# Convolution and mixture of experts on one core: a pair's result goes from ScalarE to DRAM by an adding transfer, in a new order

## The chip, the cores and the metric

The program runs on one of the eight cores of a Trainium2 chip. The metric is device time in microseconds (us) of one execution. Engines are named as in the profile: PE (TensorE, matrix products), PEld (its weight loads), DVE (VectorE), ACT (ScalarE), POOL (GpSimd), SP (SyncE, which issues most DMA transfers).

## What is computed

A causal convolution with weights that differ from token to token, and a layer of eight experts behind it, over 8 x 3584 = 28672 tokens of 192 features:

```python
w = exp(weight_gen - max); w = w / (sum(w) + 1e-9)      # 8 heads, 7 taps per token
out = einsum('bshk,bskhg->bshg', w, x_unf)              # x_unf: the 7 last tokens, 24 features a head

skip_score = x @ w_skip                                 # x is the convolution's result
do_compute = skip_score > 0
logits = x[do_compute] @ w_gate                         # 8 experts
e_idx, gate_w = argmax(logits), softmax(logits)[e_idx]
out[do_compute] = x + gate_w * (relu(x @ w1[e]) @ w2[e])    # 192 -> 1024 -> 192
```

About half of the tokens go to an expert, the others keep the convolution's result.

## The kernel before

The tokens are cut into 16 chunks of 1792. In a chunk (`chunk`), the weights are loaded, normalised by a softmax (`soft`, units so, ss, sf, sm) and written to DRAM in a skewed image, from which they come back as rows (`rot`). `band` (unit bd, L437) multiplies them with a mask into band matrices, eight in a chunk; each may be made by VectorE or by GpSimd. `conv` (cv, L452) multiplies the bands with the inputs, `conv_out` (co, L459) copies the results out, `back` and `back_out` transpose them into a tile `acc`, which goes to the result tensor `out` in DRAM (`answer`). `logits`, `choose` (begins at L501), `rank` and `place` route the tokens: each active token's number is put into a list of its expert by `list_out` (L637, L638) and `send` (L647), an indirect transfer that adds 44 short rows to a table in DRAM.

A pair is two tiles of 128 tokens of one expert. For each of the 57 pairs (`pair`, class `Pair`) the steps are: `rows` (its 256 token numbers come from the table), `index` (L802, numbers to row indices; entries without a token get an index out of bounds and are skipped), `gather` (L809, two indirect transfers from `out` to a buffer `xg`, of which there are seven), `sums`, `scales`, `high`, `low` (L844), `cross` (L850), which split the rows into two float16 parts, a transposition (by TensorE for the first twelve pairs, by DMA from SP for the others), `up` (L880, four steps), `up_high` (hh, L885, ScalarE) and `up_low` (hl, L889, VectorE), `down` (L902, four steps), and then

```python
def finish(self):                       # L907, two instructions on VectorE
    nc.vector.scalar_tensor_tensor(xg, py, fc, xg, op0=mult, op1=add)
def scatter(self, t):                   # L911, two plain indirect transfers
    nc.gpsimd.indirect_dma_start(out=..., in_=xg, ...)
```

So a pair's rows are read, changed in `xg` and written back, and `xg` is taken again when that write has landed. Forty pairs are dealt out while chunks are still running, in batches (`BATCH`: after which chunk, for which experts), nine more by what is left of whole tiles, eight for the remainders. A loop at the end takes further tiles if there are any; in this run there are none. Each expert's weights are loaded and split into two float16 parts once (`expert`; split by L361 on ScalarE and L359 on VectorE).

No instruction finds its place at run time. A planner (`Planner`, `Paced`) runs when the kernel is built: each unit has an engine or a choice of engines, an estimated length, predecessors and buffers, and the unit with the smallest start plus a kind's bias from the table `LATER` is put next; each engine then works its list in order, and waits at its head for what it needs. `E_AT` says behind which input load an expert's weights are loaded, `AHEAD`, `LEAD` and `SWITCH` how far the convolution may run ahead of the pairs.

## Time and profile before

| | us |
|---|---|
| median of 3 runs | 921.68 (918.16 to 921.82) |
| profiled execution, its own time | 921.96 |
| its span, first to last instruction | 920.3 |
| TensorE busy | 778.9 (85%) |
| VectorE busy | 692.9 (75%) |
| ScalarE busy | 441.2 (48%) |
| GpSimd busy | 435.8 (47%) |
| mean granted TensorE clock, share of full speed | 0.925 |

The shares are means over a front in which convolution, routing and the first pairs run together and a last part of pairs alone. So the views that follow are cut by time. Matmuls are pipelined: a group's mean duration is longer than the step from one matmul to the next, and the step of a pair is read from time marks.

### The profile page before, as it was taken

How to read it: one execution, taken by the hardware profiler on the slowest of the kernel's cores; microseconds unless marked ns; L12 is line 12 of the kernel's file. 1: busy time of each engine (PE TensorE's matmuls, PEld its weight loads, DVE VectorE, ACT ScalarE, POOL GpSimd, SP SyncE). 2: the span in 40 equal slices, each digit the busy share in tenths (PEclk: the TensorE clock that was granted, in tenths of full speed). 3: DMA queues.
4: the chain of work that ended last, by engine and by line, in shares of the span. 5: the costliest groups of instructions: out<-in, count | busy, mean ns of one | idle time of the engine just before them, and what ended most of it. 6: DMA issues, size and time to landing. Idle time of an engine off the chain costs nothing. (4 is left out here: it accounts for less than half of the span.)

```text
span 920.3 us, 27436 instructions
## 1 busy us (share of the span) xinstructions
PE 778.9 (85%) x11064; PEld 682.7 (74%) x11064; DVE 692.9 (75%) x1822; ACT 441.2 (48%) x1028; POOL 435.8 (47%) x496
## 2 busy tenths in 40 slices
PE   2476767687597888979988899999999999999995
PEld 1365645466475767767867789999999999999995
DVE  6678988999998979988888686765656565656552
ACT  1345445555664566545644543444444444444441
POOL 2025336317544554964676426355545454446422
PEclk9677888689878879999999999999999999999998
DMA  4789688659663685566667544333334654995220
GB/s 135 202 243 318 214 301 279 200 159 381 176 192 116 209 300 167 168 224 201 220 211 208 174 112 94 70 88 88 74 81 82 152 147 121 250 273 142 65 46 21
DMA packets 107633, 158.80 MB, mean 173 GB/s; under 512 B 65734, under 2 KB 87190, under 8 KB 104560
## 3 DMA queue, kind: packets, MB, share of 16 engines
q1 hardware_dynamic: 95280, 135.28, 49.5%
q0 software_dynamic: 12224, 21.75, 8.4%
q8 instruction: 87, 1.43, 0.6%
q14 instruction: 42, 0.34, 0.1%
HBM read 88.07 MB, written 42.37 MB: 142 GB/s over the span
## 5 line engine op out<-in xcount | busy, mean ns | idle before, releaser
L889 DVE SCALAR_TENSOR_TENSOR hl<-h,hh 128x512 f16<-128x512 f32 x228 | 155.4, 686 | 136.8 <-ACT hh L885 136.6
L885 ACT ACTIVATE hh<-h 128x512 f16<-128x512 f32 x228 | 135.7, 597 | 227.4 <-PE h L880 221.7
L880 PE MATMUL h<-xT,held 128*128 128x256 f16 x1920 | 237.3, 276 | 0.0
L880 PEld LDWEIGHTS <-held 128*128 128x128 f16 x1920 | 187.0, 99 | 25.5 <-issue 3.9
L902 PE MATMUL py<-held,hh 128*128 128x192 f16 x1536 | 205.5, 248 | 0.0
L452 PE MATMUL h<-bd,xt 128*48 128x56 f32 x4096 | 145.1, 236 | 63.0 <-DVE bd L437 36.5
L911 POOL DMA_INDIRECT out_dram<-xg,idx x114 | 118.7, 1041 | 159.2 <-DVE xg L907 138.5
L452 PEld LDWEIGHTS h<-bd,xt 128*48 128x48 f32 x4096 | 130.8, 142 | 84.9 <-DVE bd L437 42.2
L902 PE MATMUL py<-held,hl 128*128 128x192 f16 x768 | 190.3, 248 | 2.3 <-DVE hl L889 2.3
L437 POOL TENSOR_TENSOR bd<-rot,mask 128x896 f32<-128x896 f32 x57 | 112.9, 1994 | 145.0 <-PE h L452 144.5
L902 PEld LDWEIGHTS <-hh 128*128 128x128 f16 x1824 | 166.1, 98 | 6.0 <-issue 1.8
L809 POOL DMA_INDIRECT xg<-out_dram,idx x114 | 122.9, 1078 | 90.5 <-issue 52.1
L459 ACT COPY xs<-h 112x448 f32<-112x448 f32 x123 | 65.2, 532 | 109.3 <-PE h L452 107.2
L902 PEld LDWEIGHTS <-hl 128*128 128x128 f16 x912 | 89.8, 98 | 3.8 <-DVE hl L889 3.6
L437 DVE TENSOR_TENSOR bd<-rot,mask 128x896 f32<-128x896 f32 x71 | 77.1, 1118 | 9.4 <-PE h L452 5.3
L468 PE MATMUL pa<-ident,xs 112*112 112x112 f32 x512 | 76.2, 286 | 9.4 <-ACT xs L459 7.6
L482 ACT COPY acc<-pa 112x384 f32<-112x384 f32 x128 | 57.3, 480 | 38.8 <-PE pa L468 35.9
L468 PEld LDWEIGHTS pa<-ident,xs 112*112 112x112 f32 x512 | 55.4, 145 | 20.0 <-ACT xs L459 13.2
L647 POOL DMA_INDIRECT table<-ly,lri x16 | 33.5, 2091 | 48.5 <-DVE ly L638 46.3
L907 DVE SCALAR_TENSOR_TENSOR xg<-py,fc,xg 128x192 f32<-128x192 f32 x114 | 41.9, 408 | 10.6 <-PE py L902 10.6
L839 ACT ACTIVATE xs<-xg,rs 128x192 f16<-128x192 f32 x114 | 44.9, 446 | 6.3 <-DVE rs L835 6.3
L470 PE MATMUL pa<-xs,gt 112*32 112x224 f32 x512 | 39.4, 381 | 9.3 <-ACT acc L482 8.3
(191 smaller groups left out, 956.0 us busy)
## 6 DMA issues: line engine op xcount, KB each, us to landing
xt<-in_x_dram SPq DMA_DIRECT2D x64, 768.0 KB
out_dram<-acc SPq DMA_DIRECT2D x16, 1351.0 KB
acc<-held SPq DMA_DIRECT2D x9, 1536.5 KB
held<-in_moe_w_dram SPq DMA_DIRECT2D x14, 768.0 KB
rot<-img SPq DMA_DIRECT2D x15, 448.0 KB
wt<-in_weight_gen_dram SPq DMA_DIRECT2D x15, 392.0 KB
img<-wt SPq DMA_DIRECT2D x30, 196.0 KB
xg<-out_dram,idx POOLq DMA_INDIRECT x114
```

The source lines that it names most:

```text
L437: (nc.gpsimd if on_pool else nc.vector).tensor_tensor(bd.rearrange("p h (m u) -> p h m u", m=K), rot_[c][:, :, i0 * H:(i0 + 2) * H].rearra ...
L452: nc.tensor.matmul(bt_[k][g][HR * j:HR * j + 2 * G, c0:c0 + QH], xt_[k][:, b0:b0 + 2 * G], bd_[k, i // 2][:, i % 2 * H + h, :], start=True ...
L459: (nc.scalar.copy if on_act else nc.vector.tensor_copy)(xs[:, 2 * g:2 * g + 2, :], bt_[k][g][0:Q, 0:2 * QB * QH].rearrange("p (x c) -> p x ...
L468: nc.tensor.transpose(t[0:Q, x * P:x * P + Q], xs[:, x, j * Q:(j + 1) * Q], ident[0:Q, 0:Q])
L482: nc.scalar.copy(acc_[c].rearrange("p (a b) d -> p a b d", a=2)[:, :, 2 * q + j, 0:D].rearrange("p a (x g) -> p a x g", g=G), t[0:Q, :].re ...
L809: i = nc.gpsimd.indirect_dma_start(out=self.xg[:, t, :], out_offset=None, in_=out[0:n, :], in_offset=bass.IndirectOffsetOnAxis(ap=self.idx ...
L839: nc.scalar.activation(self.xs[:, t, 0, 0:D], self.xg[:, t, 0:D], AF.Copy, scale=self.rs[:, t:t + 1])
L880: nc.tensor.matmul(ph[:, fi * 2 * P:(fi + 1) * 2 * P], self.fetched()[:, a * FF + f0:a * FF + f0 + P], self.xT[:, :, cc, :], start=j == 0, ...
L885: nc.scalar.activation(self.hh[f2], self.ph[f2], AF.Relu)
L889: nc.vector.scalar_tensor_tensor(self.hl[f2], self.ph[f2], 0.0, self.hh[f2], op0=ALU.max, op1=ALU.subtract)
L902: nc.tensor.matmul(self.py[:, t, 0:D], l[:, a], w2v[:, f, r, :], start=f == 0 and t == 0 and j == 0, stop=f == NFB - 1 and j == 2, skip_gr ...
L911: i = nc.gpsimd.indirect_dma_start(out=oviews[nsc[0] % 8], out_offset=bass.IndirectOffsetOnAxis(ap=self.idx[:, t:t + 1], axis=0), in_=self ...
```

## The change

`finish` becomes two ScalarE instructions that write the product of `py` and the factor `fc` alone to a buffer `y` (three of them, their 193rd column zero), and `scatter` adds `y` to the rows in DRAM: the transfers have compute_op=add. `xg` is only read, and is free after `low` and `factor`. Entries without a token no longer have an index out of bounds: `out` gets 1152 spare rows in front (`FIRST`), which are cleared once (`clear_rows`, 889 KB); a gather reads row p of them in partition p, and an addition goes to one of eight further blocks of 128. For this `index` makes two lists on VectorE, `idx` and `put`, and the small memset that GpSimd made in front of each pair's gathers goes. `BATCH`, `E_AT`, `LATER`, `AHEAD`, `LEAD`, `SWITCH` get other values and a list `PACE` ties late bands to early pairs, so all engines' lists are in a new order.

```diff
-BATCH = [(0, 0, 2), (0, 2, 4), (3, 4, 6), (5, 6, 8), (5, 0, 2), ...
+BATCH = [(4, 0, 2), (4, 2, 4), (4, 4, 6), (6, 6, 8), (6, 0, 2), ...
-E_AT = [8, 16, 18, 26, 5, 19, 38, 37]
+E_AT = [24, 0, 31, 20, 15, 35, 0, 10]
-LATER = ({"an": -0.77, "as": 1.7, "bd": 0.87, ...
+LATER = ({"an": 3.18, "as": 0.55, "bd": 1.91, ...
-AHEAD, LEAD, SWITCH, TURN = 3, 1, 14, 12
+AHEAD, LEAD, SWITCH, TURN = 6, 4, 25, 12
...
-    for t in xgs:
-        nc.gpsimd.memset(t, 0.0)
...
+    ys = [cst.tile([P, TT, RW], F32, name=f"y{i}") for i in range(NY)]
+    for y in ys:
+        nc.vector.memset(y[:, :, D:RW], 0.0)
...
         def index(self):
-            self.idx = sl.tile([P, TT], I32, tag="idx", name="idx", bufs=XG)
-            nc.vector.tensor_scalar(self.idx, self.ids, -1.0, BIG, op0=ALU.mult, op1=ALU.add)
+            self.idx = sl.tile([P, TT], I32, tag="idx", name="idx", bufs=16)
+            nc.vector.tensor_scalar(self.idx, self.ids, which, None, op0=ALU.max)
+            self.put = sl.tile([P, TT], I32, tag="put", name="put", bufs=16)
+            nc.vector.tensor_tensor(self.put, self.ids, spare_rows[:, self.view():self.view() + TT], op=ALU.max)
 
         def gather(self, t):
             self.xg = xgs[(self.p or 0) % XG]
-            if not t:
-                nc.gpsimd.memset(self.xg[:, :, D:RW], 0.0)
...
         def finish(self):
+            self.y = ys[(self.p or 0) % NY]
             for t in range(TT):
-                nc.vector.scalar_tensor_tensor(self.xg[:, t, 0:D], self.py[:, t, 0:D], self.fc[:, t:t + 1],
-                                               self.xg[:, t, 0:D], op0=ALU.mult, op1=ALU.add)
+                nc.scalar.activation(self.y[:, t, 0:D], self.py[:, t, 0:D], AF.Copy, scale=self.fc[:, t:t + 1])
 
         def scatter(self, t):
             i = nc.gpsimd.indirect_dma_start(
-                out=oviews[nsc[0] % 8],
-                out_offset=bass.IndirectOffsetOnAxis(ap=self.idx[:, t:t + 1], axis=0),
-                in_=self.xg[:, t, :], in_offset=None, bounds_check=N - 1, oob_is_err=False)
+                out=oviews[self.view() + t],
+                out_offset=bass.IndirectOffsetOnAxis(ap=self.put[:, t:t + 1], axis=0),
+                in_=self.y[:, t, :], in_offset=None, bounds_check=FIRST + N - 1, compute_op=ALU.add)
...
+    def clear_rows():
+        nc.sync.dma_start(out[0:FIRST, :].rearrange("(p r) c -> p r c", p=P), zeros[:, 0:RW].unsqueeze(1).to_broadcast([P, FIRST // P, RW]))
...
-        add(("fi", p), "DVE", .82, o.finish, [("dn", p, 3), ("fc", p)], gives=[("y", p, 1), ("fc", p, 1)])
+        add(("fi", p), "ACT", .85, o.finish, [("dn", p, 3), ("fc", p)], takes=["yy"], gives=[("y", p, 1), ("fc", p, 1)])
...
-                size=108, gives=[("xg", p, 2)])
+                size=108, gives=[("yy", p, 2)])
...
+        for h, n in enumerate(PACE):
+            if n:
+                behind(("bd", 2 * h, 0), ("up", n - 1, 0))
```

What the lists look like. Counted in TensorE's list, 1.75 pairs' up-products stand in front of the logits of the seventh chunk and 12 in front of those of the sixteenth before; now it is none and 20.5. Of the 128 bands VectorE makes 71 and GpSimd 57 before, now 33 and 95; up to the seventh routing VectorE makes 36 of them before and 27 now. Up to VectorE's seventh routing four experts' scales stand in its list before, two now. The numbers of lines differ between the two kernels: the finish is L907 and L919, the scatter L911 and L922, a band L437 and L445, the table L647 and L655, the gather L809 and L820.

GpSimd, in the chunks near the end of the convolution, before (bands, the table's transfer, the result's, the gathers):

```order
L437 TENSOR_TENSOR bd<-rot,mask 128x896 x2
L647 DMA table<-ly,lri 3870x64
L850 COPY xs<-xs 128x2x64 x2
L911 DMA out_dram<-xg_149,idx 28672x193 x2
L437 TENSOR_TENSOR bd<-rot,mask 128x896
L807 MEMSET xg_147 128x2
L809 DMA xg_147<-out_dram,idx 128x193 x2
```

and now, at the same place:

```order
L445 TENSOR_TENSOR bd<-rot,mask 128x896
L655 DMA table<-ly,lri 3870x64
L820 DMA xg_156<-out_dram,idx 128x193 x2
L922 DMA out_dram<-y_167,put 29824x193
L445 TENSOR_TENSOR bd<-rot,mask 128x896
L922 DMA out_dram<-y_167,put 29824x193
L445 TENSOR_TENSOR bd<-rot,mask 128x896 x3
```

A pair's two result transfers now read a `y` buffer and stand between bands, the memset is gone, and there are more bands on this engine.

ScalarE, up to the last chunk's exponential (L548) before; xs are the convolution's results, acc and ls their transposed copies, hh the first part of a pair's hidden values:

```order
L459 COPY xs_7913<-h_83 112x448
L850 COPY xs<-xs 128x2x64 x2
L482 COPY acc<-pa 112x2x192 x2
L478 COPY ls<-pa 128x224
L459 COPY xs_8010<-h_84 112x448
L459 COPY xs_8010<-h_85 112x448
L885 ACTIVATE hh<-h_83 128x512
L482 COPY acc<-pa 112x2x192 x2
L478 COPY ls<-pa 128x224
L885 ACTIVATE hh<-h_84 128x512
L885 ACTIVATE hh<-h_85 128x512
L548 ACTIVATE dls<-dls 112x16x8
```

and now, in the same chunk:

```order
L467 COPY xs_9003<-h_84 112x448
L919 ACTIVATE y_165<-py,fc 128x192 x2
L490 COPY acc<-pa 112x2x192 x2
L467 COPY xs_9100<-h_85 112x448
L467 COPY xs_9100<-h_83 112x448
L486 COPY ls<-pa 128x224
L896 ACTIVATE hh<-h_84 128x512
L490 COPY acc<-pa 112x2x192 x2
L896 ACTIVATE hh<-h_85 128x512
L486 COPY ls<-pa 128x224
L467 COPY xs_9250<-h_83 112x448
L467 COPY xs_9250<-h_84 112x448
```

The finish (L919) stands among the copies, in front of the next pair's hh.

VectorE, in a chunk of the second half before, with a pair's finish (L907) behind two bands:

```order
L844 SCALAR_TENSOR_TENSOR xs<-xg_147,rs,xs 128x192 x2
L939 SCALAR_TENSOR_TENSOR sent<-base,ecap 1x8
L437 TENSOR_TENSOR bd<-rot,mask 128x896 x2
L907 SCALAR_TENSOR_TENSOR xg_150<-py,fc,xg_150 128x192 x2
L832 TENSOR_SCALAR S_7643<-S_7643 128x2
L833 TENSOR_SCALAR S_7643<-S_7643 128x2
L835 RECIPROCAL rs<-S_7643 128x2
L870 SCALAR_TENSOR_TENSOR fc<-S_6667,held,xg_153 128x2
```

and now, just ahead of a routing, with no finish and with two index lists for a pair:

```order
L855 SCALAR_TENSOR_TENSOR xs<-xg_151,rs,xs 128x192 x2
L861 COPY xs<-xs 128x2x64 x2
L813 TENSOR_SCALAR idx<-ids,which 128x2
L815 TENSOR_TENSOR put<-ids,spare_rows 128x2
L509 TENSOR_SCALAR ina<-route,noob 112x16
```

The bands and the finish have left this part of the list.

## Rows read from the trace of the kernel before

**Rows 1.** Busy us per engine in three stretches, then granted clock, DMA share, GB/s.

```profile
55.26:233.26 178.00, 131.10 (x2390) 102.72 (x2387) 160.03 (x390) 94.51 (x192) 80.51 (x81) 0.84 0.78 261
233.26:532.43 299.17, 249.83 (x4330) 208.32 (x4329) 261.13 (x630) 167.84 (x384) 170.15 (x178) 0.91 0.61 196
532.43:900.00 367.57, 365.94 (x3868) 344.86 (x3867) 230.42 (x708) 162.80 (x425) 175.35 (x206) 1.00 0.49 117
```

**Rows 2.** The same view for one window of 46 us.

```profile
414.00:460.00 46.00, 42.37 (x762) 35.68 (x762) 40.80 (x105) 27.55 (x69) 24.64 (x30) 0.96 0.66 210
```

**Rows 3.** VectorE in order of time: start us, us, line; first, seventh, sixteenth routing.

```profile
55.26 0.23 DVE L501 TENSOR_SCALAR ina<-route,noob 112x16 f32<-112x16 f32 x1
...
233.26 0.23 DVE L501 TENSOR_SCALAR ina<-route,noob 112x16 f32<-112x16 f32 x1 [0.46 <-PE route L492]
...
532.43 0.23 DVE L501 TENSOR_SCALAR ina<-route,noob 112x16 f32<-112x16 f32 x1 [0.32 <-PE route L492]
```

**Rows 4.** The same view: the finish of the 15th and of the last pair.

```profile
560.47 0.74 DVE L907 SCALAR_TENSOR_TENSOR xg<-py,fc,xg 128x192 f32<-128x192 f32 x2
...
910.35 0.74 DVE L907 SCALAR_TENSOR_TENSOR xg<-py,fc,xg 128x192 f32<-128x192 f32 x2 [1.65 <-PE py L902]
```

**Rows 5.** Chain that ended last: start us, us, what; its last piece.

```profile
912.37 0.94 POOL out_dram L911
```

**Rows 6.** Groups of instructions by form, VectorE and GpSimd: busy us, mean ns | idle before.

```profile
L889 DVE SCALAR_TENSOR_TENSOR hl<-h,hh 128x512 f16<-128x512 f32 x228 | 155.4, 686 | 136.8 <-ACT hh L885 136.6
...
L437 POOL TENSOR_TENSOR bd<-rot,mask 128x896 f32<-128x896 f32 x57 | 112.9, 1994 | 145.0 <-PE h L452 144.5
...
L437 DVE TENSOR_TENSOR bd<-rot,mask 128x896 f32<-128x896 f32 x71 | 77.1, 1118 | 9.4 <-PE h L452 5.3 <-DMA rot<-img 3.5 <-issue 0.5
...
L844 DVE SCALAR_TENSOR_TENSOR xs<-xg,rs,xs 128x192 f16<-128x192 f32 x114 | 42.9, 418 | 0.0
...
L907 DVE SCALAR_TENSOR_TENSOR xg<-py,fc,xg 128x192 f32<-128x192 f32 x114 | 41.9, 408 | 10.6 <-PE py L902 10.6
L416 DVE TENSOR_TENSOR wt<-wt,sm 112x896 f32<-112x896 f32 x30 | 41.6, 1387 | 1.0
...
L622 DVE TENSOR_TENSOR dm<-moves 44x8 f32<-44x8 f32 x16 | 14.2, 890 | 0.6
...
L850 DVE COPY xs<-xs 128x128 f16<-128x128 f16 x80 | 12.7, 236 | 1.3
L359 DVE SCALAR_TENSOR_TENSOR held<-held,wsc 128x1536 f16<-128x1536 f32 x7 | 12.6, 1806 | 0.0
...
L802 DVE TENSOR_SCALAR idx<-ids 128x2 int32<-128x2 f32 x57 | 8.7, 169 | 4.3 <-DMA ids<-table 4.3
...
L459 DVE COPY xs<-h 112x448 f32<-112x448 f32 x5 | 3.1, 614 | 2.5 <-PE h L452 2.5
```

**Rows 7.** Lines L622, L416, L437: duration ns min/median/max, first and last start.

```profile
L622 DVE TENSOR_TENSOR dm<-moves x16: 158/288/3335, 69.9 to 546.7; 44x8 f32<-44x8 f32 x16
...
L416 DVE TENSOR_TENSOR wt<-wt,sm x34: 393/1092/3524, 8.3 to 462.5; 112x896 f32<-112x896 f32 x30, 112x224 f32<-112x224 f32 x2, 112x672 f32<-112x672 f32 x2
...
L437 POOL TENSOR_TENSOR bd<-rot,mask x57: 1885/1898/2886, 56.8 to 520.0; 128x896 f32<-128x896 f32 x57
```

**Rows 8.** Indirect transfers on GpSimd, min/median/max ns: the adding one, the plain scatter.

```profile
L647 POOL DMA_INDIRECT table<-ly,lri x16: 1476/1739/3822, 71.6 to 548.8; - x16
...
L911 POOL DMA_INDIRECT out_dram<-xg,idx x114: 970/1007/2078, 230.8 to 912.3; - x114
```

**Rows 9.** Waits of the whole span: us in total, times, longest us.

```profile
PEld h L452 <- DVE bd L437: 42.2, 12, 18.0
PE h L452 <- DVE bd L437: 36.5, 6, 18.0
```

**Rows 10.** Groups by form, ScalarE: busy us, mean ns | idle before, and what ended it.

```profile
L885 ACT ACTIVATE hh<-h 128x512 f16<-128x512 f32 x228 | 135.7, 597 | 227.4 <-PE h L880 221.7 <-issue 3.4 <-PE py L902 1.4
...
L839 ACT ACTIVATE xs<-xg,rs 128x192 f16<-128x192 f32 x114 | 44.9, 446 | 6.3 <-DVE rs L835 6.3
```

More of the change, by code (lines that the diff above doesn't have):

```diff
@@ L50 @@
 TT = 2
+NY = 3
+FIRST = 9 * P
 XG, XT, WT, BD, ACC, XS = 7, 2, 1, 3, 2, 3
 LAST_F = 9
[L53 removed]
+BATCH = [(4, 0, 2), (4, 2, 4), (4, 4, 6), (6, 6, 8), (6, 0, 2), (6, 2, 4), (6, 4, 6), (8, 6, 8), (9, 0, 4), (11, 4, 8), (11, 0, 4), (11, 4, 8), (13, 0, 4), (14, 4, 8)]
 STATIC = sum(b - a for _, a, b in BATCH)
@@ L278, in conv_moe_kernel @@
     nc.vector.tensor_copy(which, which_i)
+    spare_rows = cst.tile([P, 8], F32, name="spare_rows")
+    spare_i = cst.tile([P, 8], I32, name="spare_i")
+    nc.gpsimd.iota(spare_i, pattern=[[P, 8]], base=P, channel_multiplier=1)
+    nc.vector.tensor_copy(spare_rows, spare_i)
     xgs = [cst.tile([P, TT, RW], F32, name=f"xg{i}") for i in range(XG)]
-    for t in xgs:
-        nc.gpsimd.memset(t, 0.0)
     mask = cst.tile([P, K, U], F32, name="mask")
@@ L636, in list_out @@
         y = li_[c] = st.tile([LR, LC], F32, tag="ly", name="ly")
-        nc.vector.tensor_scalar(y, li[0:LR, 0:LC], 0.0, BIG + 1 - c * CH, op0=ALU.is_gt, op1=ALU.mult)
-        nc.vector.tensor_tensor(y, y, li[0:LR, 0:LC], op=ALU.subtract)
+        nc.vector.tensor_scalar(y, li[0:LR, 0:LC], 0.0, float(FIRST - 1 + c * CH), op0=ALU.is_gt, op1=ALU.mult)
+        nc.vector.tensor_tensor(y, y, li[0:LR, 0:LC], op=ALU.add)
     sp_, nu_, li_, bg_, routed = {}, {}, {}, {}, []
     def answer(c):
-        return nc.sync.dma_start(out[c * CH:(c + 1) * CH, :].rearrange("(p b) d -> p b d", b=NB), acc_[c])
+        return nc.sync.dma_start(out[FIRST + c * CH:FIRST + (c + 1) * CH, :].rearrange("(p b) d -> p b d", b=NB), acc_[c])
     def send(c):
@@ L1034, in pair @@
             issued=[("fr", p - 1)], takes=["xg"], size=60, gives=[("bs",) + SHARED[p]] if p in SHARED else [])
-        add(("id", p), "DVE", .18, o.index, [("fr", p)])
+        add(("id", p), "DVE", .34, o.index, [("fr", p)])
         for t in range(TT):
-            add(("gr", p, t), "POOL", 1.17 if t else 1.3, lambda t=t: o.gather(t), [("id", p)], issued=[("gr", p, t - 1), ("gr", p - 1, 1)], size=108)
+            add(("gr", p, t), "POOL", 1.17, lambda t=t: o.gather(t), [("id", p)], issued=[("gr", p, t - 1), ("gr", p - 1, 1)], size=108)
         if e is None:
@@ L1043, in pair @@
         add(("ph", p), "ACT", .8, o.high, [("p2", p)])
-        add(("p3", p), "DVE", .83, o.low, [("ph", p)])
+        add(("p3", p), "DVE", .83, o.low, [("ph", p)], gives=[("xg", p, 2)])
         add(("p4", p), ("DVE", "ACT", "POOL"), (.35, .6, .9), o.cross, [("p3", p)])
@@ L1053, in pair @@
         add(("fc", p), "DVE", .21, o.factor, whole + [("p2", p)], issued=[("fc", p - 1)], takes=["fc"],
-            gives=[("S1", p, 1)] + ([("acc", ("fw", p), 2)] if e is None else []))
+            gives=[("S1", p, 1), ("xg", p, 2)] + ([("acc", ("fw", p), 2)] if e is None else []))
         for f in range(NFB // 2):
@@ L1108, in conv_moe_kernel @@
         add(("tz",), "SP", .5, clear_table, size=995)
+        add(("ty",), "SP", .4, clear_rows, issued=[("tz",)], size=100)
         for c in range(NCHUNK):
```

18 lines of the change are left out of this document (9 added, 9 removed), and 27 rows, old and new, of the table LATER.

## The prediction, made before the changed kernel ran

> **What bounds the kernel now.** I read the busy shares by stretch first, then the time marks, then the waits. One mark cuts the run: L501, with which VectorE begins the routing of a chunk; its first, seventh and sixteenth occurrence stand at 55.26, 233.26 and 532.43 us [rows 3]. Between them lie stretch A (178.0 us, almost only convolution and routing) and stretch B (299.2 us, convolution with pairs between); behind them is stretch C, pairs alone.
>
> [rows 1] shows three different limits. In A VectorE is busy 160.0 of 178.0 us (90%) and TensorE 131.1. In B VectorE is busy 261.1 of 299.2 us (87%) and TensorE 249.8 (83%), so VectorE sets the pace and TensorE comes close behind. In C TensorE is busy 365.9 of 367.6 us and VectorE 63%. The waits agree for A and B: what TensorE waits for is bands, 36.5 us by its matmuls and 42.2 by its weight loads [rows 9], and bands are made by VectorE and GpSimd. C runs at a fixed step: from the finish of the 15th pair to that of the 57th it is 910.35 - 560.47 = 349.9 us for 42 pairs, 8.33 us each [rows 4].
>
> So the time is A, B, and the pairs that B left over. By the order of TensorE 12 of 57 pairs have their up-products in front of the sixteenth routing; 532.4 + 45 x 8.33 = 907.3. The profiled execution took 921.96 us (median of the three runs 921.68, so the profile is typical); the remaining 14.7 us are the turn into C, the tail and what lies outside the span, and I keep them.
>
> **What the change moves out of VectorE.** Part by part, with means from [rows 6]:
> The finish (L907, 408 ns, two in a pair) leaves VectorE, 0.82 us a pair. In C this is worth nothing, because TensorE is at 99.6% there. In A and B it counts. The second index adds one small instruction a pair, priced like the first (L802, 169 ns). The order of bands is the larger part: of 128 bands VectorE made 71 and GpSimd 57, now VectorE makes 33 and GpSimd 95.
>
> Stretch A, now up to the same seventh routing: nine bands fewer on VectorE (9 x 1.118 = -10.1); the preparation of two experts' weights now lies behind A (three splits of which the largest takes 1.806 us, and their scales: about -11.5 in all); four more copies of convolution results (4 x 0.614 = +2.5); four fewer hl (4 x 0.686 = -2.7); the rest cancels to about -0.2. Sum -22.0. At the old share of 90% the 160.0 - 22.0 = 138.0 us take 153.5, and the mark falls at 55.3 + 153.5 = 208.8. DMA has to keep up: its share was 0.78 in A [rows 1]. The same work in 153.5 us would be 0.90, less what belonged to the two experts; the spare rows are cleared in here too, once. This fits, but without slack.
>
> Stretch B holds 20.5 pairs instead of 10.25 (12 less the 1.75 that lay in A). VectorE: 29 bands fewer (-32.4); 22 finishes fewer (-9.0); 38 more hl (x 0.686 = +26.1); 14 more low halves (L844, x 0.418 = +5.9); 42 more half-exchanges on VectorE (L850, x 0.236 = +9.9); 8 more copies (x 0.614 = +4.9); 34 more indices (x 0.169 = +5.7); the two experts, +11.5; small ones, scales, factors, two more softmax folds and assignments, about +13. Sum +35.6, so 296.7 us of VectorE for twice the pairs. At the old 87.3% this is 340 us.
>
> TensorE in B: the old 249.8 less 10.25 x 8.33 = 85.4 for the pairs leaves 164.4 for nine chunks; now 164.4 + 20.5 x 8.33 = 335 us. That is as much as VectorE has, so both are near full. The best earlier window of both is [rows 2]: TensorE 42.37 and VectorE 40.80 of 46, that is 0.92 and 0.89 at once. At 0.92 TensorE takes 364 us.
>
> **What it puts elsewhere.** Bands on GpSimd hold VectorE up. L622, an operation on 8 columns with two operands in SBUF, takes 158 ns at best, 288 in the median and 3335 at most; L416 1092 in the median and 3524 at most; a band on GpSimd holds at least 1.885 us [rows 7]. Lower bound of the price: the excess of these two lines, 16 x (890 - 158) ns and 30 x (1387 - 1092) ns by their means [rows 6], is 20.5 us for 57 bands, 0.36 us a band. Upper bound: every band stops VectorE for its whole 1.885 us. I take 0.36, since most of VectorE's time in B goes to hl, which reads PSUM and spread little. It gives 8 x 0.36 = 3 us in A and 30 x 0.36 = 11 us in B, over the shares +3 and +12.
>
> [...]
>
> ScalarE takes the finish. Nearest row: L839, 128x192 with a scale, 446 ns [rows 10]; two of them 0.89 us a pair. In B ScalarE was busy 167.8 of 299.2; with 40 to 44 single finishes (20) and 34 to 38 more hh (x 0.597 = 20 to 23) it comes to 210, and with the moved preparation of two experts to some 225 of 358. In C it goes from 44% to 55%. Hidden in both; what queues behind a finish is hh of the next pair, for which VectorE waits, and three h banks and ScalarE's long wait for TensorE (221.7 us before hh) cover 0.9 us.
>
> GpSimd: seven starting memsets and one of 2 columns in each pair go (nothing waits for them), 38 bands come (38 x 1.994 = 76 us) and the result goes out by an adding transfer. No row shows an adding transfer of this size. Near ones: the plain one of the same 128 rows, 970 to 1007 ns, and the adding one of 44 short rows into the table, 1476 at least, 1739 in the median, 3822 at most [rows 8]. So 1.0 to 3.8 us; I take 1.5 to 2.1, since the adding row is alike in kind and most of its spread falls in busy stretches. In B GpSimd then has 61 bands (121), 48 gathers (priced as the scatter's 1.007: 48), 44 additions (66 to 92), nine tables and small work (some 38): 273 to 299 of 358 us. In C a pair costs 2 x 1.007 + 2 x 2.1 = 6.2 of 8.33. Covered, but GpSimd takes its work in order: a band behind an addition waits for ScalarE's finish, and TensorE for the band. In exchange a buffer of gathered rows no longer waits for its scatter to land, and the three y buffers give an addition two pairs' time (over 16 us in C) to land, against 7.0 us from the end of the last scatter's issue to the end of the span [rows 5]; so that wait should hide.
>
> Tail: finish, two issues, landing stay. Two issues instead of 0.98 us each cost +1 to +2.2; the reading of the old rows adds between 0 and another 7.0 us of landing. I take +2.
>
> **The sum.** A ends at 208.8 + 3 = 212. B lies between VectorE's 340 + 12 = 352 and TensorE's 364: 358. The sixteenth routing is then at 570. Left are 57 - 20.5 = 36.5 pairs, 304.0 us; with 14.7 and 2 the end is at **891 us**, 31 us (3.3%) less. In words: 8.5 pairs (71 us) move out of C, and the front gets 38 us longer for them.
>
> **Rivals.**
> Bands lock VectorE (slower). Mechanism: each band moved to GpSimd stops VectorE for its 1.885 us. For: L622 and L416 at their maxima. Against: medians near the minimum. Price: 38 x 1.885 = 72 us instead of 14, and 58 over a share of 0.88 is +66, so 957 us. It turns slower from 1.1 us a band on. Chance 0.05.
> The addition is dear on GpSimd (slower). From (8.33 - 2.01) / 2 = 3.16 us an issue on, GpSimd sets the step of C. At the maximum of 3.82 a pair takes 9.65 us, 36.5 x 1.32 = +48, so 939 us. For: 44 rows already cost 1.5. Against: the row includes disturbed ones. Chance 0.06.
> The two engines don't overlap better (slower). TensorE keeps its old 83.5% in B, because bands, copies and hl wait for each other across in-order queues: 335 / 0.835 = 401, +43, so 934 us. For: the waits for bands in [rows 9], and more bands behind transfers. Against: the window at 0.92. Chance 0.06; half-way to it, B at 389, the gain is gone (922, within 0.5%): 0.07.
> The change gives all it could: no new stops and TensorE in B as full as in C (335 / 0.996): B is bound by VectorE's 340, the end at 549 + 304 + 14.7 + 1 = 869 us. Chance 0.06, counted with faster.
> That the pairs come no earlier can be left out: the order fixes it.
>
> **How the numbers follow.** The forecast's own band, 873 to 917, holds 0.70, the full gain 0.06; together 0.76 faster. Below 0.5% (4.6 us, about what a measurement of this kernel can tell from no change) 0.07; slower 0.17. The range runs from 868 (full gain) up to 924, where B takes 391 us or GpSimd's additions 3.3 us in C; less than 2 in 10 lies outside. I set 891.
>
> **What would show it.** The seventh routing near 212 us and the sixteenth near 570, with TensorE above 0.9 between; 36 or 37 pairs at 8.33 us behind it; the adding issue at 1.5 to 2.1 us; L622's mean not far above 890 ns; VectorE's total down by some 70 us. Wrong would be: pairs in the last stretch above 8.4 us (GpSimd), B above 389 us with TensorE at 0.84 or less (coupling), L416 and L622 at several us each (locks), or DMA above 0.95 in A.

## The result

The changed kernel took 934.82 us (median of four executions, 930.93 to 935.34), the kernel before beside it 921.08: 1.0146 times as long, 95% interval 1.0111 to 1.0182. So it is slower by 13.7 us, where I had said 891 us and a gain of 31. The profiled execution spans 933.1 us.

In the later comparisons (all but e1, e2, e5 and e6) the kernel before took 946 to 958 us in place of 921, also on a chip of the same number as in the first ones, so runs are compared by their ratio to the kernel before that ran beside them, and traces, where there is one, with the trace of a mate from such comparisons.

First the three marks, VectorE in order of time (start us, us, line; the routing is now L509), which answer to [rows 3]:

```profile
54.93 0.23 DVE L509 TENSOR_SCALAR ina<-route,noob 112x16 f32<-112x16 f32 x1
...
220.56 0.21 DVE L509 TENSOR_SCALAR ina<-route,noob 112x16 f32<-112x16 f32 x1
...
614.01 0.23 DVE L509 TENSOR_SCALAR ina<-route,noob 112x16 f32<-112x16 f32 x1
```

Then the three stretches between and behind them, answering to [rows 1] (busy us of PE, PEld, DVE, ACT, POOL, then granted clock, DMA share, GB/s):

```profile
54.93:220.56 165.63, 122.72 (x2307) 94.63 (x2304) 148.88 (x363) 77.33 (x162) 96.16 (x85) 0.84 0.72 247
220.56:614.01 393.45, 333.31 (x5149) 281.89 (x5148) 319.10 (x795) 213.29 (x486) 275.60 (x218) 0.90 0.66 181
614.01:900.00 285.99, 284.08 (x3009) 267.74 (x3007) 162.72 (x479) 162.73 (x460) 167.12 (x126) 1.00 0.67 130
```

The seventh routing comes at 220.6 (I had 212) and the sixteenth at 614.0 (I had 570). Stretch A is 12.4 us shorter than before, B is 94.3 us longer, and what lies behind the sixteenth routing went from 387.9 to 319.1 us, 68.8 less. So 81.9 us were paid in front for 68.8 behind. Stretch C is as forecast: ScalarE's finish has the old step, 915.59 - 674.00 = 241.59 us for 29 pairs, 8.33 each (compare [rows 4]).

```profile
674.00 0.73 ACT L919 ACTIVATE y<-py,fc 128x192 f32<-128x192 f32 x2 [0.40 <-PE py L913]
...
915.59 0.73 ACT L919 ACTIVATE y<-py,fc 128x192 f32<-128x192 f32 x2 [0.39 <-PE py L913]
```

The whole error lies in A and B: 559.1 us against 514.7. TensorE's work in B is what I had worked out (333.3 against 335), but it fills 84.7% of the stretch and not 92%, and VectorE is busy 468.0 us in the two where I had 448.7.

Now the groups by form that answer to [rows 6] (busy us, mean ns | idle before):

```profile
L445 POOL TENSOR_TENSOR bd<-rot,mask 128x896 f32<-128x896 f32 x95 | 186.5, 2029 | 131.7 <-PE h L460 131.1
L922 POOL DMA_INDIRECT out_dram<-y,put x114 | 182.5, 1600 | 110.0 <-ACT y L919 86.2 <-issue 12.6 <-ACT hh L896 6.0
...
L855 DVE SCALAR_TENSOR_TENSOR xs<-xg,rs,xs 128x192 f16<-128x192 f32 x114 | 65.4, 614 | 4.5 <-ACT xs L850 4.2
L919 ACT ACTIVATE y<-py,fc 128x192 f32<-128x192 f32 x114 | 41.6, 419 | 22.8 <-PE py L913 22.3 <-issue 0.4
...
L424 DVE TENSOR_TENSOR wt<-wt,sm 112x896 f32<-112x896 f32 x29 | 33.0, 1138 | 0.9
...
L630 DVE TENSOR_TENSOR dm<-moves 44x8 f32<-44x8 f32 x16 | 8.5, 533 | 0.6
```

The two lines from which I had taken the price of a band became shorter: L416 (now L424) went from 1387 to 1138 ns, L622 (now L630) from 890 to 533. The low half of a gathered tile (L855, L844 before) went from 418 to 614 ns, though nothing in it has changed. Its shortest, median and longest durations, and those of the adding issue (answering to [rows 7] and [rows 8]), show why:

```profile
L855 DVE SCALAR_TENSOR_TENSOR xs<-xg,rs,xs x114: 391/412/6968, 204.1 to 894.4; 128x192 f16<-128x192 f32 x114
...
L922 POOL DMA_INDIRECT out_dram<-y,put x114: 1541/1570/2393, 250.9 to 925.4; - x114
```

Half take 412 ns or less, and the longest takes 6968. That one stands at 462 us. Three engines in order of time there (start us, us; at a row's end the idle time before it), GpSimd, VectorE and TensorE:

```profile
462.68 6.16 POOL L445 TENSOR_TENSOR bd<-rot,mask 128x896 f32<-128x896 f32 x3
```

```profile
462.10 7.30 DVE L855 SCALAR_TENSOR_TENSOR xs<-xg,rs,xs 128x192 f16<-128x192 f32 x2
469.43 0.30 DVE L861 COPY xs<-xs 128x128 f16<-128x128 f16 x2
469.64 1.28 DVE L900 SCALAR_TENSOR_TENSOR hl<-h,hh 128x512 f16<-128x512 f32 x2
```

```profile
458.19 0.33 PE L913 MATMUL py<-held,hh 128*128 128x192 f16 x2
...
465.20 0.34 PE L913 MATMUL py<-held,hh 128*128 128x192 f16 x2
470.38 0.34 PE L913 MATMUL py<-held,hl 128*128 128x192 f16 x1 [4.84 <-DVE hl L900]
470.51 0.53 PE L913 MATMUL py<-held,hh 128*128 128x192 f16 x2
```

GpSimd makes three bands one after another, 462.68 to 468.84 us. For that whole time VectorE stands in two operations that need 0.8 us together. An hl (the low half of a pair's hidden values) waits behind them in VectorE's list, and TensorE, whose list is in order too, waits 4.84 us for the hl. Afterwards two matmuls of the same line take 0.53 us in place of 0.33, up to 474 us. The granted clock, 1.00 in the 3 us from 465 on, is 0.50 from 470 to 474 us; in the mean of the 12 us from 465 on it is 0.72 (columns as in the stretches above):

```profile
465.00:477.00 12.00, 7.16 (x92) 5.91 (x86) 8.34 (x9) 1.48 (x4) 3.84 (x3) 0.72 0.43 76
```

At 462 us the hold lasted as long as a run of three bands, 6.16 us. It was paid in VectorE's time and again in TensorE's wait, and the lower clock came behind that wait; that the wait brought the clock down is how I read this one place, no run shows it. So the price of a hold is not the mean of its own line.

TensorE's longest waits in B (us in total, times, longest us) are for small VectorE operations on a chain:

```profile
PE pm L344 <- DVE wd L342: 13.1, 6, 4.6
PE route L552 <- DVE pf L531: 9.3, 3, 5.3
PE py L913 <- DVE hl L900: 7.5, 5, 4.8
...
PE h L460 <- POOL bd L445: 5.0, 5, 2.0
```

So the bands themselves are hardly waited for in B. What is waited for are the scales of an expert's weights (wd), the routing (pf) and hl, which VectorE finishes late.

### The profile page after: what moved, and what is told of

The parts are those of the page before. It is cut to its first block, busy times and chain, and to the rows that moved or that the text cites. A ratio compares the mean times of both kernels' runs of the same rounds, so it can differ in the third digit from the quotient of the medians.

```text
span 933.1 us, 27459 instructions
## 1 busy us (share of the span) xinstructions
PE 782.9 (84%) x11064; PEld 681.1 (73%) x11064; DVE 673.9 (72%) x1736; ACT 475.5 (51%) x1148; POOL 554.2 (59%) x458
## 3 DMA queue, kind: packets, MB, share of 16 engines
q0 software_dynamic: 23168, 22.73, 16.0%
## 4 chain that ended last, share of the span: by engine, by line
PE 51%; DVE 27%; issue 7%; DMA 5%; ACT 5%; POOL 5%; POOLq 0%; DVEq 0%; ACTq 0%; SPq 0%
PE h L891 20%; PE py L913 18%; PE h L460 7%; DMA out_dram<-y,put 3%; POOL bd L445 2%; PE pa L476 2%; DVE hl L900 2%; DVE xs L855 2%; DVE bd L445 2%; PE pa L478 1%; DMA xt<-in_x_dram 1%; DVE sp L605 1%; DVE held L367 1%; DVE fold L410 1%; POOL out_dram L922 1%
## 5 line engine op out<-in xcount | busy, mean ns | idle before, releaser
L445 POOL TENSOR_TENSOR bd<-rot,mask 128x896 f32<-128x896 f32 x95 | 186.5, 2029 | 131.7 <-PE h L460 131.1
L900 DVE SCALAR_TENSOR_TENSOR hl<-h,hh 128x512 f16<-128x512 f32 x228 | 154.9, 689 | 147.3 <-ACT hh L896 145.4
L922 POOL DMA_INDIRECT out_dram<-y,put x114 | 182.5, 1600 | 110.0 <-ACT y L919 86.2
L891 PE MATMUL h<-xT,held 128*128 128x256 f16 x1920 | 242.8, 280 | 5.0 <-DMA held<-wlo 4.3
L460 PE MATMUL h<-bd,xt 128*48 128x56 f32 x4096 | 139.2, 233 | 56.9 <-DVE bd L445 34.0
L820 POOL DMA_INDIRECT xg<-out_dram,idx x114 | 132.5, 1162 | 81.3 <-DVE put L815 41.3
L460 PEld LDWEIGHTS h<-bd,xt 128*48 128x48 f32 x4096 | 127.1, 140 | 72.9 <-DVE bd L445 41.5
L467 ACT COPY xs<-h 112x448 f32<-112x448 f32 x111 | 58.8, 531 | 106.6 <-PE h L460 101.9
L913 PEld LDWEIGHTS <-hl 128*128 128x128 f16 x912 | 90.5, 99 | 12.4 <-DVE hl L900 11.9
L490 ACT COPY acc<-pa 112x384 f32<-112x384 f32 x128 | 56.6, 479 | 54.1 <-PE pa L476 52.5
L855 DVE SCALAR_TENSOR_TENSOR xs<-xg,rs,xs 128x192 f16<-128x192 f32 x114 | 65.4, 614 | 4.5 <-ACT xs L850 4.2
L919 ACT ACTIVATE y<-py,fc 128x192 f32<-128x192 f32 x114 | 41.6, 419 | 22.8 <-PE py L913 22.3
L655 POOL DMA_INDIRECT table<-ly,lri x16 | 26.5, 1654 | 34.7 <-DVE ly L646 14.1
```

What stands on the lines that cost most here:

```text
L445: (nc.gpsimd if on_pool else nc.vector).tensor_tensor(bd.rearrange("p h (m u) -> p h m u", m=K), rot_[c][:, :, i0 * H:(i0 + 2) * H].rearra ...
L460: nc.tensor.matmul(bt_[k][g][HR * j:HR * j + 2 * G, c0:c0 + QH], xt_[k][:, b0:b0 + 2 * G], bd_[k, i // 2][:, i % 2 * H + h, :], start=True ...
L467: (nc.scalar.copy if on_act else nc.vector.tensor_copy)(xs[:, 2 * g:2 * g + 2, :], bt_[k][g][0:Q, 0:2 * QB * QH].rearrange("p (x c) -> p x ...
L490: nc.scalar.copy(acc_[c].rearrange("p (a b) d -> p a b d", a=2)[:, :, 2 * q + j, 0:D].rearrange("p a (x g) -> p a x g", g=G), t[0:Q, :].re ...
L820: i = nc.gpsimd.indirect_dma_start(out=self.xg[:, t, :], out_offset=None, in_=out[0:n, :], in_offset=bass.IndirectOffsetOnAxis(ap=self.idx ...
L855: nc.vector.scalar_tensor_tensor(xs[:, t, 1, 0:D], self.xg[:, t, 0:D], self.rs[:, t:t + 1], xs[:, t, 0, 0:D], op0=ALU.mult, op1=ALU.subtract)
```

## Experiments

Four theories. **L**: bands on GpSimd hold VectorE longer than the 0.36 us that I took. **C**: more pairs between the routings cannot be overlapped, whatever holds VectorE. **K**: the new code (finish on ScalarE, adding transfers) costs time itself. **I**, formed on the way: TensorE's idle time in A and B is constant, so that pairs in front save nothing.

### Code or order

The planner's tables were exchanged first.

```diff
e1, on the changed kernel:
-BATCH, E_AT, LATER, AHEAD ... = (the changed kernel's), PACE = [...]
+BATCH, E_AT, LATER, AHEAD ... = (those of before), PACE = []
e2, on the kernel before: the other way round
```

> The changed code (finish on ScalarE, adding transfers, spare rows) with the tables of the kernel before (BATCH, E_AT, LATER, AHEAD; no PACE). VectorE makes 77 bands and GpSimd 51 (71 and 57 before, 33 and 95 after), 11.75 pairs stand ahead of the 16th logits (12 before, 20.5 after). Theory K, the loss lies in the new code itself (dearer issues on GpSimd, a finish on ScalarE that holds hh): 930 us or more. Theory L, it lies in the 38 bands moved to GpSimd and their locks: faster than the kernel before, about 912 us, since VectorE loses 0.89 us a pair and gets no more locks. Theory C, it lies in the order with more pairs between the routings: 915 to 921 us.

> The code of the kernel before with the tables of the changed one and PACE. The planner, with the finish still on VectorE, gives VectorE 51 bands and GpSimd 77 and puts 13 pairs ahead of the 16th logits. Theory L at 0.8 us a moved band: 20 more bands on GpSimd take 20 x 0.8 = 16 us of VectorE's gain and 8 us come back in shorter stretch C, about 928 us. Theory C: about 921 us, since the pairs in front are hardly more. Theory K: 921 us or less.

Measured: 974.12 us, 1.0607 (1.0529 to 1.0685), and 998.17 us, 1.0827 (1.0768 to 1.0886). Both are far worse than either kernel, which none of the theories had. In e1 A and B together take 476.3 us, as before (477.2), and the part behind takes 430.0 instead of 387.9. The tables belong to the units' costs and buffers: with other costs the planner makes an order that nobody chose. These two say nothing on code or order. The clean form keeps the planner's input, and with it the order, and changes only what a unit issues:

```diff
e8, on e1: the unit costs and buffer rules of before, the changed code
-add(("fi", p), "ACT", .85, o.finish, ..., takes=["yy"], gives=[...])
+add(("fi", p), "DVE", .82, o.finish, ..., gives=[...])
-            size=108, gives=[("yy", p, 2)])
+            size=108, gives=[("xg", p, 2)])
...
e9, on e2: the costs and rules of the changed kernel, the code of before
```

> The changed code in exactly the sequence of the kernel before: the planner is given the tables and the unit costs of before, so every unit stands where it stood (71 bands on VectorE, 57 on GpSimd, 12 pairs ahead of the 16th logits), and only what the units issue is the changed code's. If the loss lies in the code (theory K): 935 us or more. If it lies in the new sequence (theories L and C): between 912 us (the finish gone from VectorE for the 12 pairs of the stretches it limits, 12 x 0.8 us) and 921 us.

> The code of before in exactly the sequence of the changed kernel (33 bands on VectorE, 95 on GpSimd, 20.5 pairs ahead of the 16th logits), with 11 gather buffers in place of 7, which that sequence needs as the finish still writes into them. If the loss lies in the sequence (L and C): 935 us or more, up to 945 us, since VectorE has the finish of 20.5 pairs on top (20.5 x 0.5 us). If it lies in the code (K): 921 us or less.

Measured: e8 0.9833 (0.9758 to 0.9908), e9 1.0228 (1.0176 to 1.0280; it has 11 gather buffers in place of 7). In these comparisons K falls: in either order the new code is the better one (in the new order narrowly, 1.0228 against 1.0146), and the new order is what costs. As e8 beats the kernel before, it was run again beside the changed kernel, and a third time below.

> The changed kernel once more, beside the next three on one chip, since the kernel before took 921 us in one comparison and 958 in another. Every theory: 1.5% slower than the kernel before, as measured first.

> The changed code in exactly the sequence of the kernel before, once more, beside the changed kernel itself. If the code is a gain and the new sequence a loss: 1 to 2% faster than before and about 3% faster than the changed kernel. If the 1.7% of the first time belonged to that chip: within 0.5% of before.

Measured: the changed kernel 1.0136 (1.0085 to 1.0187), e8 0.9883 (0.9843 to 0.9922), 937.72 against 960.31 us. All of this stems from comparisons in which the kernel before takes 946 us or more. Where it takes 921, e8 was not run, and none of e8's medians (937.72 to 943.20 us) lies below 921; so the gain of the code alone, and the fall of K, are not shown for the 13.7 us of the first comparison. The traces tell where e8 wins. e11 and e13 below have the code and the sequence of before behind the sixteenth routing; they took 402.6 and 397.0 us there, the three runs of e8 390 to 392. But the first trace of the kernel before has 387.8 us there, and it has 477.2 us in A and B, where e8 takes 486 to 489. So e8 wins in the last stretch, over a kernel before that is slow in it. The changed kernel too is slow there in the later comparison (335.5 us against 319.1). Its VectorE has stops for which the profile names no other engine ("issue"; 2.6 us in the first trace):

```profile
DVE hl L900 <- issue: 24.0, 20, 1.8
```

e8 has as many (24.9 us) and yet keeps 8.25 us a pair. Why is open.

Two parts of the code alone:

```diff
e3, on the changed kernel:
-nc.scalar.activation(self.y[...], self.py[...], AF.Copy, scale=self.fc[...])
+nc.vector.tensor_scalar(self.y[...], self.py[...], self.fc[...], None, op0=ALU.mult)
e18, on e8:
-in_=self.y[:, t, :], ..., compute_op=ALU.add)
+in_=self.y[:, t, :], ...)
```

> The changed kernel with the finish made by VectorE at the same place in the order (two multiplications of 128x192, about 0.4 us each). VectorE has 17 us more in the first two stretches. If VectorE's amount of work sets them: 12 to 19 us slower than the changed kernel, 1.03 of before. If it doesn't, as the run with light hl points to: within 5 us of the changed kernel, 1.010 to 1.020; faster, 1.005, if the finish on ScalarE delayed hh.

> The changed code in the sequence of before with plain transfers in place of adding ones (the addition of a pair's result to its row is left out, rows are overwritten). Its mate took 0.985 of before. If the adding form is dear (theory K): each issue falls from 1.57 to 1.0 us and the packets by half, 5 us or more gained, below 0.980. If its price is hidden beside TensorE: 0.982 to 0.988.

Measured: e3 1.0230 (1.0174 to 1.0285), 0.9% or some 8 us worse than the changed kernel (the intervals touch): half of the 17 us that VectorE gets. e18 1.0253 (1.0214 to 1.0293), which is slower than its mate with additions (0.985), and no theory had that. An issue takes 1041 ns in the mean against 1616, so the adding form is dearer on GpSimd as I had it; its price is hidden (e8 keeps its 8.25 us a pair with it). The loss of e18 lies behind the sixteenth routing (413.9 us against 391.6), where TensorE is busy longer for the same 3970 matmuls:

```profile
553.44:959.30 405.86, 386.74 (x3970) 353.36 (x3968) 213.46 (x665) 187.23 (x519) 173.64 (x169) 0.99 0.46 109
```

```profile
547.50:931.10 383.60, 377.11 (x3970) 353.13 (x3968) 213.73 (x665) 191.24 (x519) 227.72 (x170) 1.00 0.62 115
```

(first e18, then e8 as run the third time). TensorE also stands still there for 11.4 us in 24 stops for which the profile names no other engine, in e8 for 0.6 us. So it is not shown that the loss comes from the plain form; its cause is open.

### What a band on GpSimd costs

```diff
e5, on the kernel before, behind two of every three GpSimd bands:
+nc.gpsimd.tensor_tensor(extra..., rot_[c]..., mask..., op=ALU.mult)
e11, at the same places:
+nc.gpsimd.memset(extra, 0.0)
+nc.gpsimd.memset(extra, 0.0)
```

> The kernel before, with 38 more bands made by GpSimd into a tile that nobody reads (two behind every third of its own). Nothing else is changed, so VectorE keeps its work and only the locks and GpSimd's 1.9 us each are added. GpSimd has 196 us free in the second stretch, VectorE next to nothing. Locks at 0.36 us a band, as in the prediction: about 921 + 14 = 935 us. Locks at 0.8 us: about 951 us. At 1.885 us, the whole band: 990 us. No lock price (theory C or K): 921 to 925 us.

> The control for the run with 38 more bands, which took 955 us: at the same 38 places of the kernel before GpSimd makes two fills of 128x1088 fp32 (about 0.9 us each, 1.8 us in all), which read nothing, in place of a band. If the 34 us came from VectorE being held while GpSimd reads and writes a band: 921 to 928 us here. If they came from GpSimd being late for its other work, or if a fill holds VectorE too: 945 to 955 us; the two are told apart by VectorE's durations in the trace.

Measured: e5 954.97 us, 1.0410 (1.0328 to 1.0492). (GpSimd's free time in B of the kernel before is 299.17 - 170.15 = 129.0 us by [rows 1], not 196.) Its two stretches:

```profile
54.56:244.97 190.41, 134.18 (x2383) 104.94 (x2380) 172.16 (x390) 94.86 (x195) 118.83 (x96) 0.81 0.76 248
244.97:565.23 320.26, 253.37 (x4329) 209.48 (x4329) 287.04 (x629) 166.70 (x379) 217.46 (x200) 0.89 0.56 180
```

Nobody reads the 38 bands, and A and B take 510.7 us instead of 477.2: 0.88 us a band. With the same instructions VectorE is busy 730.8 us in place of 692.9, 1.0 us a band. That is L, at nearly three times my price. e11: 1.0142 (1.0064 to 1.0221), a third of the loss; VectorE's busy time is 707.5 us, 0.38 us for each pair of fills (2.0 us of GpSimd). So most of the price belongs to bands and not to GpSimd's time as such. A band reads two operands and a fill none; that this makes the difference is not shown.

The holds can also be added up inside one trace, without a mate: for each VectorE operation in A and B, its duration less the median of those of its line and shape that overlap no GpSimd instruction. The operations that overlap a band are too long by 46.5 us in the kernel before (57 bands) and by 77.4 us in the changed kernel (95 bands), 0.8 us a band in both; all others together by 0.5 and 5.0 us. In e5 it is 85.0 us. In e11 the operations that overlap a fill and no band are too long by 6.6 us, 0.17 us for each pair of fills.

Then the 38 bands themselves, at the same places of an order that stays:

```diff
e6, on the changed kernel (e17 on e8, with "DVE" and "POOL" exchanged, 71 for 95):
+if u.kind[0] == "bd" and u.engine == "POOL":
+    turns += 1
+    if turns * 38 // 95 > (turns - 1) * 38 // 95:
+        u.engine = "DVE"
```

> The changed kernel with 38 of the 95 GpSimd bands made by VectorE at the same place in the order (71 and 57, as before the change); the pairs ahead of the 16th logits stay 20.5. VectorE gets 38 x 1.1 us = 42 us of work and loses the locks of 38 bands. Theory L: at a price of 1.1 us a band or more it is as fast as the changed kernel (935 us) or faster; at 0.8 us 935 + 38 x 0.3 = 946 us; at 0.36 us 963 us. Theory C: VectorE in the second stretch goes from 319 to 361 us of work, so about 960 us. Theory K says nothing of this run.

> The changed code in the sequence of before with one thing moved: 38 of VectorE's 71 bands are made by GpSimd at the same place (33 and 95, as in the changed kernel); 12 pairs stay in front. It is the bands alone, without the rest of the new order. Its mate without the move took 0.985 of before. If a moved band costs VectorE less than its own 1.1 us (0.36 us, as in the prediction): 38 x 0.7 = 28 us less VectorE work, 8 to 28 us faster, 0.955 to 0.977. If it costs as much as it saves: 0.985. If the bands are what costs the 39 us by which the new order is worse at 12 pairs in front: 1.01 to 1.025.

Measured: e6 940.02 us, 1.0232 (1.0182 to 1.0283); by its trace it spans 932.4 us against 933.1, and its A and B take 558.7 against 559.1. e17 1.0258 (1.0228 to 1.0289), against e8's 0.985. Its stretches A and B, then those of e8 (third run):

```profile
60.93:256.23 195.30, 134.15 (x2414) 105.30 (x2412) 165.85 (x380) 95.05 (x193) 113.26 (x91) 0.82 0.73 242
256.23:574.85 318.62, 253.50 (x4310) 211.37 (x4306) 261.22 (x603) 173.48 (x406) 218.06 (x183) 0.90 0.59 181
```

```profile
58.84:239.66 180.82, 133.80 (x2415) 104.90 (x2413) 158.20 (x394) 95.82 (x197) 84.06 (x78) 0.84 0.80 261
239.66:547.50 307.84, 252.47 (x4314) 209.80 (x4314) 248.56 (x620) 172.72 (x401) 180.13 (x162) 0.91 0.61 187
```

The two stretches are 25.3 us longer. VectorE gave 38 bands away, 38 x 1.097 = 41.7 us of its own work, and is busy 18.9 us more over the span (675.1 against 656.2). It is held 61 us more, 1.6 us a band. In e6 VectorE took back 38 x 1.13 = 43 us of work and was busy only 8.8 us more (682.7 against 673.9 in the span): 0.9 us a band. So a moved band cost 0.9 to 1.6 us where it saved 1.1. In the new order it is worth next to nothing, in the old one it is a loss.

The holds can also be taken away from all bands:

```diff
e10, on the changed kernel (e13 the same on the kernel before):
-bd = st.tile([P, 2 * H, QH], F32, tag="bd", ...)
+bd, n = bds[(2 * k + j) % BD], 2 if on_pool else 2 * H
 (nc.gpsimd if on_pool else nc.vector).tensor_tensor(bd[:, 0:n]..., op=ALU.mult)
```

> The changed kernel where each of GpSimd's 95 bands writes 2 of its 16 heads (the other 14 stay zero, that part of the convolution is left out), in three lasting buffers that are filled with zeros once. The number of instructions and their order stay. Theory L: the locks of 95 bands go from about 0.9 us to 0.15 us each, 70 us less on VectorE in the first two stretches; the second stretch falls to what TensorE needs, 333 us of work, some 350 us in all, and the kernel to 880 to 895 us. If locks are 0.36 us a band: 95 x 0.3 = 28 us at most, 910 to 920 us. If GpSimd and its locks are nothing (theory C alone): 925 to 935 us.

> The kernel before where each of its 57 bands on GpSimd writes 2 of 16 heads (that part of the convolution is left out; the routing then sees other values, so only the first two stretches can be compared, not the number of pairs at the end). Its mate, the changed kernel with light bands, needed 521 us for the first two stretches, 38 less than with whole bands. If the locks of the bands make the whole difference between the two sequences, the light kernel of before saves less: 57 x 0.9 = 51 us of VectorE at most, 20 to 25 us of time, 453 us for both stretches, and with the 8.5 pairs more that it leaves (71 us) it would be 3 us worse than its mate. If the order costs time even without locks: it saves as much as its mate or more, 440 us or less, and stays 10 us or more better.

e10 was 0.9861 (0.9816 to 0.9905), e13 0.9711 (0.9666 to 0.9756); with other routing behind, only A and B are compared, first of e10, then of e13:

```profile
53.37:210.55 157.18, 116.68 (x2304) 90.56 (x2301) 130.60 (x362) 76.78 (x162) 52.66 (x85) 0.89 0.77 260
210.55:574.35 363.80, 326.63 (x5154) 277.92 (x5152) 264.46 (x795) 212.47 (x487) 183.00 (x218) 0.94 0.70 196
```

```profile
56.65:228.53 171.88, 132.38 (x2384) 104.03 (x2381) 145.81 (x390) 94.12 (x192) 47.91 (x84) 0.85 0.82 274
228.53:518.00 289.47, 247.53 (x4338) 204.51 (x4337) 232.83 (x629) 167.15 (x384) 120.42 (x174) 0.94 0.63 200
```

With light bands the changed order needs 521.0 us for A and B, 38 less than with whole ones in the first trace and 47 less than in that of the later comparison (567.7); the order of before needs 461.4, 16 less than in its only trace. L had asked for some 350 us in B of e10, and it was 363.8. The difference between the orders falls from 81.9 to 59.6 us, and 8.5 pairs behind cost 8.5 x 8.33 = 70.8. By this estimate the change would have been worth 11 us without the bands' time; with it, it costs 11. The whole runs do not bear it out: e10's ratio lies 1.5% above e13's, since e10 takes 369.8 us behind the sixteenth routing, with 58 pairs in all in place of 57 and 9.5 us for each of the last 28. Why is open. (e13 ran where the kernel before is slower than in its trace, so its saving is rather larger than 16.) For VectorE the 57 old bands cost 421.2 - 378.6 = 42.5 us, 0.75 each.

### VectorE's work, and the pairs in front

```diff
e12, on the changed kernel (hls: three lasting tiles):
-nc.vector.scalar_tensor_tensor(self.hl[f2], self.ph[f2], 0.0, self.hh[f2], ...)
+nc.vector.scalar_tensor_tensor(self.hl[f2][:, 0:64], self.ph[f2][:, 0:64], 0.0, self.hh[f2][:, 0:64], ...)
e14, on the changed kernel (e16 on e8, with 4):
+behind(("up", 12, 0), ("lg", NCHUNK - 1))
```

> The changed kernel where VectorE makes 64 of the 512 columns of each hl (the rest stays zero in three lasting tiles, so the low halves of the hidden values are left out of the result): about 0.55 us less for each of 228 instructions, 45 us less VectorE work in the second stretch (82 of its 228). If VectorE's work is what holds TensorE there (locks, or too much given to it): the second stretch goes from 393 to 350 to 365 us, the kernel to about 905 us at the pace where before takes 921. If the in-order lists and the routing's own chain hold it, whatever VectorE has to do: 385 us or more, 927 us.

> The changed kernel with the up-products of the 13th pair and all behind it held until after the 16th logits, so that 12 pairs stand in front in place of 20.5 (bands 42 and 86). Theory I (TensorE's idle time in the first two stretches is some 100 us whatever is put between, and a pair in front costs 8.8 us there against 8.33 behind): the two stretches are 75 to 80 us shorter, the last one 71 us longer, 4 to 9 us gained, 1.005 to 1.010 of before where the changed kernel is 1.014. If pairs in front fill idle time, as the prediction had it (5.7 us each): 22 us lost, 1.037. If the number of pairs is nothing and the rest of the sequence is the fault: 1.014.

> The changed code in the sequence of before (which takes 12 pairs in front) with the up-products of the fifth pair and all behind it held until after the 16th logits, so that 4 stand in front (bands 78 and 50). Theory I: TensorE's idle time in the two stretches stays near 100 us and the time goes 0 to 5 us down or stays. If pairs in front do fill idle time, up to some number that the sequence of before does not pass: 8 pairs back cost 8 x 2 to 3 us, 16 to 24 us more.

> The changed code in exactly the sequence of the kernel before, beside the run with 4 pairs in front: 0.983 to 0.990 of before, as in two comparisons on chips where before took 949 to 958 us. If that gain came from those chips alone and before takes 921 here: 0.995 to 1.005.

Measured: e12 1.0012 (0.9971 to 1.0053). VectorE has 30 us less in A and B, and both together take 565.2 us where the changed kernel beside it took 567.7; by medians it gains 9 us (951.1 against 960.3). B is 398.0 us, so the amount of VectorE's work counts for a third at most. What e10 took away and e12 did not is the holding, together with 136 us of GpSimd's work, and e10 gained 47 us against the same trace.

e14 1.0265 (1.0218 to 1.0311), e16 1.0164 (1.0118 to 1.0210), e8 this time 0.9852 (0.9796 to 0.9907). Theory I falls. Here are A and B of e16, to be held against e8 above:

```profile
58.92:241.56 182.64, 137.81 (x2409) 108.73 (x2407) 159.76 (x394) 95.86 (x197) 85.23 (x78) 0.81 0.78 259
241.56:507.12 265.56, 191.31 (x3562) 151.30 (x3560) 226.25 (x546) 132.34 (x287) 119.08 (x104) 0.81 0.64 204
```

Eight pairs fewer in front make A and B 488.7 - 448.2 = 40.5 us shorter, 5.1 us a pair, and the end 69.5 us longer, 8.7 a pair. In the changed order it is (567.7 - 523.9) / 8.5 = 5.2 us a pair (its mate is from another comparison). So pairs in front do fill idle time, 3.6 us each in the old order and, by the ratios of e14 and its mate, 1.4 us in the new one; e14 planned nine bands back to VectorE as well, so its figure is the rougher.

## Why the prediction was wrong

**What was right.** The reading of the three stretches by their busy shares; the pairs that come forward and C's step of 8.33 us; TensorE's work in B (335, measured 333.3); the adding issue (1.5 to 2.1 us, median 1.57); GpSimd's load in B (273 to 299, measured 275.6); the finish hidden on ScalarE (0.84 us a pair); and the direction of the pairs in front, which e14 and e16 bear out.

**The first step that failed** stands under "What it puts elsewhere": the price of a band on GpSimd, "I take 0.36". It measured 0.8 us (the overlaps in both traces), 1.0 (e5), 0.9 (e6) and 1.6 (e17), where the first rival had put the point of decision at 1.1. In A and B I booked VectorE 448.7 us in 514.7, a share of 0.872; it is busy 468.0 us, and at that share the stretches would take 537. So 22 of the 44 us are VectorE's own extra time. Nearly all of it is the 38 bands: I had booked 14 us for their holds, and the overlaps grew by 30.9. The error stood in the trace before: I took two lines, L622 and L416, for the lower bound and then for the value. The price has to be added up over all lines, since the holds lay on many: after the change L855's longest is 6968 ns against a median of 412, L843's 3076 against 169, L630's 1893 against 170. hl, for whose sake I took the lower value, does spread little (L889, 627 to 693 ns; L900 now, 622 to 694), but it is 27.0 of VectorE's 261.1 us in B before and 52.5 of 319.1 now, not most of it. In A and B 29 of the new ones overlap a band, and take 665 to 693 ns; why they are spared is not shown. The 57 old bands cost 0.75 us each by e13, twice what those two lines show. After the change L844, nearly undisturbed before at 418 ns, carries the largest part, and L622 and L416, which I had named as the sign of locks, became shorter; they would not have shown it.

**The second step that failed** is the other 22 us, all of them in B (in A VectorE kept its 90%, 148.9 of 165.6 us): the share. I let both engines be near full, TensorE at 0.92 by one window of 46 us ([rows 2]). It reached 0.847, near the third rival's 83.5%. That this rival's 934 us is the time that came is partly luck: it had 401 us for B, which took 393.5, and nothing for A, which took 9 us more than I had. And its mechanism, in-order lists that wait for each other whatever holds them, is not the whole of it: with light bands TensorE reaches 0.90 and A and B take 521.0 us, near my 514.7. In e11 a pair of fills keeps GpSimd busy for 2.0 us, in e5 an added band between 300 and 330 us for 1.9 to 2.4, and only a third of the loss comes (1.0142 against 1.0410). So what makes the lists wait is for the larger part the holding itself, passed on from a small VectorE operation to TensorE, as at 462 us, where TensorE waited 4.84 us. How much of these 22 us would stay without any hold is not settled, since light bands also free GpSimd and take away the holds that the kernel before had.

**A reading that was wrong.** I took [rows 9] to say that TensorE waits for bands in A and B. Most of that wait lies before the first routing. Here is the matmuls' row for that time (0 to 55.26 us), then for A and B:

```profile
PE h L452 <- DVE bd L437: 27.8, 2, 18.0
...
PE h L452 <- DVE bd L437: 8.7, 4, 3.7
```

In B alone it is 2.1 us. So VectorE's bands were hardly waited for there before the change either, and the waits gave no support to moving them.

**What the parts come to,** by ratios one after another, all from comparisons in which the kernel before takes 946 us or more: the code alone -1.5% (e8); the bands alone +4.1% (e17); the 8.5 pairs and the rest of the order -1.2%; sum +1.4%. These do not simply add: in the new order giving the bands back is no gain either (e6), presumably because 20.5 pairs in front need VectorE time that the bands would take. The order asks for more VectorE time in front, and moving bands to GpSimd does not supply it.

## What to carry to other kernels

Here the price that GpSimd's bands had for VectorE was a sum over its operations (46.5 us in the kernel before, where two lines showed 20.5), and such a price is best measured directly: issue the work once more into a tile that nobody reads, and see what it costs, or add up in a trace by how much the operations that overlap the work are too long. VectorE's busy share held its stops as well as its work (of 468.0 us in A and B, 77.4 were the excess of operations that overlapped bands); before work is moved to a neighbour to relieve it, compare the saving with the stops that the neighbour adds. And tables tuned for one set of costs did badly with another (1.0607 in e1, 1.0827 in e2); to tell code from order, exchange the code inside a sequence that is held fixed.
